# Second half of the tokens by Strassen's seven products: an attention and MLP kernel on one core

## The chip, the cores and the metric

One core of a Trainium2 chip (trn2) runs the whole program in one launch. The metric is device microseconds of an execution, the median of several. TensorE (PE in the profile) multiplies; VectorE (DVE) and ScalarE (ACT) move, round and add; SyncE (SP) issues every DMA; GpSimd (POOL) works in the attention only.

## The reference

The attention's output, 1792 tokens of 768 numbers, goes through two layers. This is the part that the change touches:

```python
def _moe_ref(x, w1, w2, w3, w_out):      # x: 1792 x 768
    a = x @ w1                           # w1, w2: 768 x 1024
    b = x @ w2
    h = a * b @ w3                       # w3: 1024 x 1024
    return (h @ w_out).astype(np.float32)   # w_out: 1024 x 768

def _moe2_ref(x, w_in, w_out):
    h = x @ w_in                         # w_in: 768 x 2048
    g = np.maximum(0.01 * h, h)
    return (g @ w_out).astype(np.float32)   # w_out: 2048 x 768
```

The weights arrive as float64. They are read as pairs of 32-bit words.

## The kernel before

The attention fills the first 409.6 us and leaves x in DRAM (`scr`). The rest is `moe()`, twice over: the tokens are taken in two halves of T = 896 columns (4 batches of S = 448 tokens, two to a half), and everything below is kept with the tokens along the columns.

Exact products come from a split. Every operand is kept as a rounded part hi (`hi_act`, one ScalarE copy) and the rest lo (`lo_dve`, one VectorE subtraction), and each 128-row block of a product is three matmuls: hi·hi, hi·lo, lo·hi. `mm` (its matmul is L619) does this for one block of 128 rows of a weight matrix against all k blocks, in the two column parts of `PARTS`, 512 and 384 columns. Each part is one PSUM bank; there are 8 banks for everything.

One half of the tokens is these stages:

- w1 and w2: 8 row blocks m each, 6 k blocks. A block of w1 and the same block of w2 make a block of h = a·b (copy on ScalarE, L684; product on VectorE, L686).
- w34: the product of w3 and w_out, made once in the first half by `fold` (L530) and stored in DRAM. 6 row blocks of 8 k blocks turn h into x2.
- four groups f: four row blocks of w_in (6 k blocks) make g with the leaky relu (L702, L704), and then the second product (L716) with four row blocks of w_out2: 14 PSUM tiles (7 row groups t of 128 tokens, 2 column halves) of 12 matmuls of 384 columns. They are added up on VectorE in `acc` (L723), and after the last f each t is stored to `out`.

The weights flow through one list, `plan`, which holds the order of all blocks for both halves. `fill` issues loads up to three ahead (buffers `wr`), `convert` turns float64 words into float32 (one ScalarE operation, four on VectorE: L92, L93, L96, L99; buffers `wc`, two), and `split` makes hi and lo (`ws`). A weight block needed in both halves is loaded as float64 and converted twice. While the last second product of the first half runs, `next_x` loads x of the second half and splits it.

Within `moe()` a scheduler orders the instructions of each engine. SyncE's queue is in order: a DMA that waits for a buffer holds those behind it.

Of the kernel before, what the change touches and what calls it, by code (L numbers as in the profile page):

```python
# [8 lines left out]
F32 = mybir.dt.float32  # L9
# [13 lines left out]
def attention_moe_kernel(ctx: ExitStack, tc, qt, kt, vt, w_pre, w_post, w1, w2, w3t, w_out, w_in2, w_out2, out):  # L23
# [37 lines left out]
    w34 = dram.tile([DF, DM], F32, name="w34")  # L61

# [23 lines left out]
    def convert(pool, t, shape):  # L86

        c = pool.tile([P, *shape], U32, tag="wc", name="wc", bufs=2)
# [392 lines left out]
    def moe():  # L481
        with ExitStack() as es:
            xp = es.enter_context(tc.tile_pool(name="m_x", bufs=1, reuse_waits="tile"))
            cv = es.enter_context(tc.tile_pool(name="m_cv", bufs=2, reuse_waits="tile"))
            wp = es.enter_context(tc.tile_pool(name="m_raw", bufs=3, reuse_waits="tile"))
            sp = es.enter_context(tc.tile_pool(name="m_split", bufs=3, reuse_waits="tile"))
            hg = es.enter_context(tc.tile_pool(name="m_hg", bufs=1, reuse_waits="tile"))
            ap = es.enter_context(tc.tile_pool(name="m_acc", bufs=1, reuse_waits="tile"))
            so = es.enter_context(tc.tile_pool(name="m_so", bufs=4, reuse_waits="tile"))
            wk = es.enter_context(tc.tile_pool(name="m_wk", bufs=2, reuse_waits="tile"))  # L490

            KM, KF, KF2 = DM // P, DF // P, DF2 // P
            T = 2 * S
            NT = T // P
            NH = DM // 2
            FQ = 4
            XREADS, XMARKS = (-5, -3), (-5, -5, -4, -4, -4, -4, -3, -3, -3, -2, -2, -2)
            PARTS = ((0, 512), (512, T - 512))

            def behind(mark):  # L500
                es = ExitStack()
                for e in mark.values():
                    es.enter_context(tc.issue_after(e.ins))
                return es

            wos = {}

            def wo_parts(kk):

                if kk < 4:  # L510
                    t = so.tile([P, 2, DM], F32R, tag="ws", name="wo")
                    wos[kk] = t[:, 0], t[:, 1]
                    return wos[kk]
                if kk == 4:
                    t = ap.tile([P, NT, DM], F32R, tag="acc", name="wo")
                    extra = ap.tile([P, DM], F32R, tag="wx", name="wo")
                    for i in range(4, KF):
                        wos[i] = t[:, 2 * i - 8], (t[:, 2 * i - 7] if i < KF - 1 else extra)
                return wos[kk]

            def fold():

                for f in range(KF):
                    wt = next_w()
                    for hf in range(2):
                        cs = slice(hf * NH, (hf + 1) * NH)
                        pw = bank([P, NH], "pw")
                        for kk in range(KF):
                            for j, (x, y) in enumerate(((0, 0), (0, 1), (1, 0))):
                                nc.tensor.matmul(  # L530
                                    pw, wt[:, x, kk, :], wos[kk][y][:, cs],
                                    start=(kk == 0 and j == 0), stop=(kk == KF - 1 and j == 2),
                                )
                        o = wk.tile([P, NH], F32, tag="at", name="wfo")
                        nc.scalar.activation(out=o, in_=pw, func=ACTF.Copy)
                        nc.sync.dma_start(out=w34[f * P:(f + 1) * P, cs], in_=o)

            def col_block(w, m):
                return w[:, 2 * m * P:2 * (m + 1) * P].rearrange("(k p) m -> p k m", p=P)

            def load_w(kind, m):
                if kind == "w34":
                    t = wp.tile([P, KF, P], F32, tag="wr", name="wf", bufs=3)
                    nc.sync.dma_start(out=t, in_=w34[:, m * P:(m + 1) * P].rearrange("(k p) m -> p k m", p=P))
                    return t
                if kind == "wf":
                    return load_raw(wp, w_out[m * P:(m + 1) * P, :].unsqueeze(1), (1, DM), 3)
                if kind == "wo":
                    return load_raw(wp, w_out2[m * P:(m + 1) * P, :].unsqueeze(1), (1, DM), 3)
                if kind == "w3t":  # L550
                    f, i = divmod(m, 2)
                    rows = w3t[i * KF // 2 * P:(i + 1) * KF // 2 * P]
                    return load_raw(wp, col_block(rows, f), (KF // 2, P), 3)
                w = {"w1": w1, "w2": w2, "wi": w_in2}[kind]
                return load_raw(wp, col_block(w, m), (KM, P), 3)

            def ready_w(kind, m, t):
                if kind == "w34":
                    shape, cf = (KF, P), t
                else:  # L560
# [38 lines left out]
            def prepare(ahead):  # L599
                while len(ready) < ahead and pos[1] < len(plan):  # L600
                    fill()
                    if not loaded:
                        return
# [177 lines left out]
```

## Time and profile before

| | |
|---|---|
| median of 3 runs | 1294.88 us (1294.81 to 1299.5) |
| the profiled execution's own time | 1296.19 us |
| its span, first to last instruction | 1294.4 us |
| TensorE busy | 1279.2 us, 99% of the span |
| TensorE weight loads busy (beside the matmuls) | 1127.2 us, 87% |
| VectorE busy | 867.4 us, 67% |
| ScalarE busy | 601.9 us, 46% |
| moved by DMA | 211.57 MB, mean 163 GB/s |

The profiled execution ran 1.3 us longer than the median; 1.8 us of its time lie outside the span. A share of busy time is a mean over the whole program; what an engine does in one stage is read from a table of windows.

### The profile page before, as it was taken

The page shows a single profiled execution, that of the slowest core. Times are in us where ns is not written, and L with a number is a line of the kernel's source. Part 1 is how long each engine was busy: PE and PEld are TensorE (multiplying, and loading weights), DVE is VectorE, ACT ScalarE, POOL GpSimd, SP SyncE. Part 2 cuts the span into 40 slices and gives each one's busy share as a digit, 9 for nine tenths or more (in the row PEclk, how much of TensorE's full clock was granted, in tenths as well). Part 3 has the DMA queues.
Part 4 walks back from the last instruction along what each step waited for, and adds up shares of the span by engine and source line. Part 5 has one row for each costly group of instructions (what it writes and reads, how often), then busy time and mean ns, then how long its engine had stood idle before and what let it go on. Part 6 is the DMA issues. An engine that isn't in the chain of part 4 may idle for free.

```text
span 1294.4 us, 22410 instructions
## 1 busy us (share of the span) xinstructions
PE 1279.2 (99%) x8926; PEld 1127.2 (87%) x8926; DVE 867.4 (67%) x1441; ACT 601.9 (46%) x1169; POOL 117.3 (9%) x192
## 2 busy tenths in 40 slices
PE   7899999999999999999999999999999999999998
PEld 5577777777778989999899999999898889999998
DVE  4565675675668999833485969695673459687662
ACT  5665666676655554522254524352332236434240
POOL 1232232232321000000000000000000000000000
PEclk8899999999999999999999999999999999999999
DMA  7998988988885654733334423363321424342302
GB/s 221 302 319 228 268 261 268 285 266 226 256 261 168 185 163 142 228 115 88 123 105 140 126 95 122 98 218 127 119 82 49 133 77 149 98 147 74 123 1 86
DMA packets 132072, 211.57 MB, mean 163 GB/s; under 512 B 19393, under 2 KB 115649, under 8 KB 131521
## 3 DMA queue, kind: packets, MB, share of 16 engines
q1 hardware_dynamic: 131969, 210.15, 52.6%
q8 instruction: 71, 1.16, 0.4%
q14 instruction: 32, 0.26, 0.1%
HBM read 157.43 MB, written 52.69 MB: 162 GB/s over the span
## 4 chain that ended last, share of the span: by engine, by line
PE 96%; DMA 3%; DVE 1%; ACT 0%; issue 0%; SPq 0%; DVEq 0%
PE pm L619 45%; PE po L716 18%; PE po L304 11%; PE pm L261 6%; PE px L324 6%; PE pw L530 5%; PE pq L203 4%; DMA sr<-sdr 2%; DMA vs<-in_v_dram 1%; PE turn L242 1%; DMA sdr<-s 0%; DVE wc L96 0%; DVE x L75 0%; ACT s L211 0%; DVE ap L311 0%
## 5 line engine op out<-in xcount | busy, mean ns | idle before, releaser
L619 PE MATMUL pm<-x,ws 128*128 128x512 f32 (+1 forms) x2304 | 467.0, 364 | 0.2 <-ACT ws L72 0.2
L619 PEld LDWEIGHTS pm<-x,ws 128*128 128x128 f32 x2304 | 417.6, 188 | 48.0 <-ACT ws L72 0.3
L716 PE MATMUL po<-ws,g 128*128 128x384 f32 x1344 | 234.3, 334 | 0.0
L716 PEld LDWEIGHTS po<-ws,g 128*128 128x128 f32 x1344 | 233.1, 188 | 0.0
L304 PE MATMUL po<-kr,e 128*112 128x120 f32 (+1 forms) x1440 | 159.7, 270 | 0.0
L277 ACT ACTIVATE e<-pm,mx 128x448 f32<-128x448 f32 x180 | 111.8, 632 | 100.0 <-DVE mx L270 99.6
L304 PEld LDWEIGHTS po<-kr,e 128*112 128x112 f32 x1440 | 151.2, 178 | 7.5 <-issue 6.3
L75 DVE TENSOR_TENSOR ws<-wc,ws 128x768 fp32r<-128x768 f32 (+1 forms) x112 | 102.5, 918 | 69.6 <-ACT ws L72 69.0
L72 ACT ACTIVATE ws<-wc 128x768 fp32r<-128x768 f32 (+1 forms) x112 | 90.8, 813 | 113.6 <-PE po L716 73.9
L91 ACT ACTIVATE wc<-wr 128x768 f32<-128x768 f32 (+1 forms) x120 | 104.9, 877 | 78.0 <-DVE ws L75 57.5
L290 POOL TENSOR_SCALAR kr<-kpost,rc 128x120 f32<-128x120 f32 x180 | 113.1, 644 | 276.2 <-DVE rc L287 144.4
L311 DVE COPY ap<-po 112x480 f32<-112x480 f32 (+1 forms) x129 | 83.8, 653 | 55.8 <-PE po L304 55.4
L270 DVE TENSOR_REDUCE mx<-pm 128x1 f32<-128x448 f32 x180 | 101.2, 618 | 25.0 <-PE pm L261 24.6
L619 PE MATMUL pm<-h,ws 128*128 128x512 f32 (+1 forms) x576 | 116.3, 363 | 0.0
L619 PEld LDWEIGHTS pm<-h,ws 128*128 128x128 f32 x576 | 104.3, 188 | 11.7
L99 DVE SCALAR_TENSOR_TENSOR wc<-wr,wc 128x768 uint32<-128x768 uint32 (+1 forms) x120 | 110.3, 920 | 1.6
L96 DVE SCALAR_TENSOR_TENSOR wc<-wr,wc 128x768 uint32<-128x768 uint32 (+1 forms) x120 | 110.0, 919 | 0.9
L261 PE MATMUL pm<-sr,kpre 60*64 60x448 f32 (+1 forms) x720 | 86.0, 567 | 7.0 <-DMA sr<-sdr 6.9
L92 DVE TENSOR_SCALAR wc<-wc 128x768 f32<-128x768 f32 (+1 forms) x120 | 64.8, 540 | 37.9 <-ACT wc L91 37.4
L324 PEld LDWEIGHTS px<-ap,vs 112*64 112x64 f32 x1536 | 73.9, 137 | 17.1 <-ACT e L277 8.2
L723 DVE TENSOR_TENSOR acc<-po,acc 128x384 f32<-128x384 f32 x84 | 46.2, 557 | 62.1 <-PE po L716 61.3
L211 ACT ACTIVATE s<-pq 120x448 f32<-120x448 f32 (+1 forms) x180 | 84.1, 560 | 4.7 <-PE pq L203 4.0
(54 smaller groups left out, 952.8 us busy)
## 6 DMA issues: line engine op xcount, KB each, us to landing
sr<-sdr SPq DMA_DIRECT2D x176, 210.0 KB
wr<-in_moe_w_out_dram SPq DMA_DIRECT2D x40, 768.0 KB
sdr<-s SPq DMA_DIRECT2D x33, 840.0 KB
wr<-in_moe_w_dram SPq DMA_DIRECT2D x32, 768.0 KB
wr<-in_moe_w_in_dram SPq DMA_DIRECT2D x32, 768.0 KB
wr<-in_moe_w_dram SPq DMA_DIRECT2D x16, 512.0 KB
sdr<-s SPq DMA_DIRECT2D x12, 616.0 KB
wf<-w SPq DMA_DIRECT2D x12, 512.0 KB
```

The source lines that it names most:

```text
L75: nc.vector.tensor_tensor(out=dst, in0=src, in1=hi.bitcast(F32), op=ALU.subtract)
L91: nc.scalar.activation(out=cf, in_=hi.bitcast(F32), func=ACTF.Abs)
L96: nc.vector.scalar_tensor_tensor(out=c, in0=hi, scalar=0xC0000000, in1=c, op0=ALU.bitwise_and, op1=ALU.bitwise_or)
L99: nc.vector.scalar_tensor_tensor(out=c, in0=lo, scalar=29, in1=c, op0=ALU.logical_shift_right, op1=ALU.bitwise_or)
L261: nc.tensor.matmul(pms[n][g * Q:(g + 1) * Q], kpre[rows], sr[rows, g, :], start=True, stop=True)
L270: nc.vector.tensor_reduce(out=mxs[n], in_=pms[n], axis=AX.X, op=ALU.max, negate=True)
L277: ends["act"] = nc.scalar.activation(out=ets[n], in_=pms.pop(n), func=ACTF.Exp, bias=mxs.pop(n), scale=1.0, accum_out=sm[:, i:i + 1])
L290: ends["pool"] = nc.gpsimd.tensor_scalar(out=kr[:, i], in0=kpost, scalar1=rc[:, i:i + 1], scalar2=None, op0=ALU.mult)
L304: nc.tensor.matmul(po[:, jc].rearrange("p h (g i) -> p h g i", g=2), e[:, jc * JP:(jc + 1) * JP], kr, start=True, stop=True,)
L324: nc.tensor.matmul(px[e * D:(e + 1) * D, r, :ni], vst[b][:, jc, 2 * p + e, :], ap[:, jc, 2 * p + e, :ni], start=(jc == 0), stop=(jc == NJ ...
L619: nc.tensor.matmul(dst, wt[:, a, kk, :], x[:, kk, c, c0:c0 + w], start=(kk == 0 and j == 0), stop=(kk == kn - 1 and j == 2),)
L716: nc.tensor.matmul(po, g[:, m, a, t * P:(t + 1) * P], wts[m][:, c, 0, cs], start=(m == 0 and j == 0), stop=(m == FQ - 1 and j == 2),)
```

## The change

Of the second half only, the products with w1, w2 and w_in are done by Strassen's scheme in the form with fifteen additions. Weights are taken as 2 x 2 blocks: two row blocks m0, m1 by two halves of the k blocks (3 each). x is taken as 2 x 2 blocks: two halves of the k blocks by the two batches of 448 columns. `seven` makes seven products of 3 k blocks (9 matmuls of 448 columns) where the plain way needs eight. Four of the seven multiply sums: S1 to S4 of weight blocks and t1 to t4 of x blocks. The seven results are put together by seven additions on VectorE (`partial`, `put_block`).

Where these sums come from: those of w1 and w2 are made in the first half, beside the w34 stage (`four_sums` on float32 blocks read back from DRAM, stored again to `summed`). Those of w_in are made in the second half on VectorE, inside the stages that multiply with w_in. The sums of x are made beside the last second product of the first half, those of x2 beside the w34 stage of the second half.

The first half now stores each converted block of w1, w2, w_in and w_out2 as float32 (`kept`, 48 stores of 393 KB), and the second half loads those and converts nothing. `convert` has three buffers `wc` for two. Second half: w34 and the second products keep their number of matmuls; w34 is taken in parts of 448 and 448 columns. A weight tile `w7` of the new scheme holds 7 blocks in hi and lo and has 2 buffers; the first half's pools are closed and the second half's opened inside the last second product.

The diff, cut to its core (the first half is indented and otherwise as it was, apart from the lines shown):

```diff
-        c = pool.tile([P, *shape], U32, tag="wc", name="wc", bufs=2)
+        c = pool.tile([P, *shape], U32, tag="wc", name="wc", bufs=3)
...
+                    if kind in kept:
+                        nc.sync.dma_start(out=kept[kind][m], in_=cf.rearrange("p k m -> p (k m)"))
...
+        def four_sums(u, a11, a12, a21, a22):
+            tt(u[:, 0], a21, a22, ALU.add)
+            tt(u[:, 2], a11, a21, ALU.subtract)
+            tt(u[:, 1], u[:, 0], a11, ALU.subtract)
+            tt(u[:, 3], a12, u[:, 1], ALU.subtract)
...
                 for m in range(KM):
                     wt = next_w()
+                    for part in PARTS:
+                        put(xx[m], mm(wt, h, KF, part), *part)
+                    for kind, m0 in (pairs.pop(0) for _ in range(min(len(pairs), 2 - m // 2 % 2))):
+                        a, u = (so.tile([P, 4, KH * P], F32, tag="ws", name=n) for n in ("sa", "su"))
+                        for i in range(2):
+                            nc.sync.dma_start(out=a[:, 2 * i:2 * i + 2], in_=halves_of(kind, m0 + i * KF // 2))
+                        four_sums(u, *(a[:, i] for i in range(4)))
+                        nc.sync.dma_start(out=summed[kind, m0], in_=u)
...
+                def weights(kind, m0, m1):
+                    w = wb.tile([P, 7, 2, KH, P], F32R, tag="w7", name="w7", bufs=2)
+                    ws = w.rearrange("p i x k m -> p i x (k m)")
+                    raw = ws[:, :, 1].bitcast(F32)
+                    for i, m, k in ((A22, m1, 1), (A11, m0, 0), (A12, m0, 1)):
+                        nc.sync.dma_start(out=raw[:, i], in_=halves_of(kind, m)[:, k])
+                    if (kind, m0) in summed:
+                        u = raw[:, 3:]
+                        nc.sync.dma_start(out=u, in_=summed[kind, m0])
+                    else:
+                        u = swp[0].tile([P, 4, KH * P], F32, tag="sw", name="sw")
+                        nc.sync.dma_start(out=u[:, 2], in_=halves_of(kind, m1)[:, 0])
+                        four_sums(u, raw[:, A11], raw[:, A12], u[:, 2], raw[:, A22])
+                    for s, r in ((raw[:, :3], slice(0, 3)), (u, slice(3, 7))):
+                        hi_act(ws[:, r, 0], s)
+                        lo_dve(ws[:, r, 1], s, ws[:, r, 0])
+                    return w
...
+                def product(w, i, b):
+                    dst = bank([P, S], "pp")
+                    for kk in range(KH):
+                        for j, (a, c) in enumerate(TERMS):
+                            nc.tensor.matmul(dst, w[:, i, a, kk, :], b[:, kk, c, :], ...
...
+                def seven(w, b, put_block):
+                    x1 = product(w, A11, b11)
+                    nc.scalar.activation(out=p1, in_=x1, func=ACTF.Copy)
+                    x5 = product(w, S1, t1)
+                    put_block(0, 0, product(w, A12, b21), p1)
+                    u2 = partial("u2", product(w, S2, t2), p1)
+                    u4 = partial("u4", x5, u2)
+                    u3 = partial("u3", product(w, S3, t3), u2)
+                    put_block(1, 1, x5, u3)
+                    put_block(1, 0, product(w, A22, t4), u3)
+                    put_block(0, 1, product(w, S4, b22), u4)
...
+                            seven(ready.pop(0), x, put_a)
+                            ahead(2 if m < KF // 2 - 1 else 1)
+                            seven(ready.pop(0), x, put_h)
...
+                    for m in range(FQ // 2):
+                        seven(ready.pop(0), x2, put_g)
```

How it moves instructions is shown at three places. In the rows after the change, line numbers are those of the changed kernel: L805 is the matmul of `product`, L515 that of `mm`, L79 makes lo (`lo_dve`), L543 is an addition or subtraction (`tt`), L537 the addition to `acc`, L944 the leaky relu; `pp` is a PSUM tile of `product`, `t_...` the sums of x, `b_...` its plain blocks, `w_...` a weight tile `w7`.

TensorE, second half: before, the first blocks of w1 and w2 (and all 32 such rows up to the w34 stage).

```order
L619 MATMUL pm<-x,ws 128x512 x18
L619 MATMUL pm<-x,ws 128x384 x18
L619 MATMUL pm<-x,ws 128x512 x18
L619 MATMUL pm<-x,ws 128x384 x18
```

And now the third weight tile of w1 and w2; 8 tiles make this stage, 8 more the w_in stages.

```order
L805 MATMUL pp<-b_9096,w_9481 128x448 x9
L805 MATMUL pp<-t_9099,w_9481 128x448 x9
L805 MATMUL pp<-b_9097,w_9481 128x448 x9
L805 MATMUL pp<-t_9100,w_9481 128x448 x9
L805 MATMUL pp<-t_9101,w_9481 128x448 x9
L805 MATMUL pp<-t_9102,w_9481 128x448 x9
L805 MATMUL pp<-b_9098,w_9481 128x448 x9
```

Two row blocks were 4 groups of 18; they are 7 groups of 9, so 63 matmuls of 448 columns for 72 of 448 on average.

VectorE, from the last second product of the first half to the first products of the second: before.

```order
L75 TENSOR_TENSOR x<-x 128x448 x3
L723 TENSOR_TENSOR acc<-po,acc 128x384
L75 TENSOR_TENSOR x<-x 128x448
L75 TENSOR_TENSOR ws<-wc,ws 128x768
L96 SCALAR_TENSOR_TENSOR wc<-wr,wc 128x768
...
L723 TENSOR_TENSOR acc<-po,acc 128x384 x3
L75 TENSOR_TENSOR ws<-wc,ws 128x768
L92 TENSOR_SCALAR wc<-wc 128x768
L93 TENSOR_SCALAR wc<-wc 128x768
L686 TENSOR_TENSOR ht<-pm,at 128x512
```

The same place now, its last rows up to the first addition of a product.

```order
L537 TENSOR_TENSOR acc<-po,acc 128x384
L79 TENSOR_TENSOR t_9102<-gt,t_9102 128x448
L79 TENSOR_TENSOR w_9472<-w_9472 128x4x384
L537 TENSOR_TENSOR acc<-po,acc 128x384 x2
L79 TENSOR_TENSOR t_9101<-gt,t_9101 128x448
...
L79 TENSOR_TENSOR t_9100<-u_9183,t_9100 128x448
L543 TENSOR_TENSOR gt<-b_9097,u_9183 128x448
L537 TENSOR_TENSOR acc<-po,acc 128x384 x2
L79 TENSOR_TENSOR b_9097<-b_9097 128x3x448
L79 TENSOR_TENSOR w_10185<-w_10185 128x1024
L79 TENSOR_TENSOR t_9102<-gt,t_9102 128x448
L543 TENSOR_TENSOR u_9430<-pp,p_9396 128x448
```

The 12 splits of x became 12 sums (L543), 12 splits of sums (L79, 448 wide) and 3 splits of plain blocks (3x448 wide), and the last of them stands directly ahead of the first product's addition.

VectorE in the stage of w_in, third group f: before, a stretch of one row block.

```order
L704 TENSOR_TENSOR gg<-pm,gt 128x512
L93 TENSOR_SCALAR wc<-wc 128x768
L75 TENSOR_TENSOR ws<-wc,ws 128x768
L96 SCALAR_TENSOR_TENSOR wc<-wr,wc 128x768
L75 TENSOR_TENSOR g<-gg,g 128x512
```

Now, at the end of the first of the group's two weight tiles.

```order
L543 TENSOR_TENSOR gt<-pp,u_11564 128x448
L79 TENSOR_TENSOR g<-gt,g 128x448
L944 SCALAR_TENSOR_TENSOR gt<-gt 128x448
L543 TENSOR_TENSOR sw<-sw,w_11727 128x384
L543 TENSOR_TENSOR sw<-w_11727,sw 128x384
L543 TENSOR_TENSOR sw<-sw,w_11727 128x384
L79 TENSOR_TENSOR g<-gt,g 128x448
L543 TENSOR_TENSOR sw<-w_11727,sw 128x384
L79 TENSOR_TENSOR w_11727<-w_11727 128x3x384
L543 TENSOR_TENSOR gt<-pp,p_11631 128x448
```

The four sums of the next group's weights (`sw`) stand in VectorE's order between the steps that make g. They need loads that SyncE can issue only when the tile `w_11727` reuses is free, that is after the last matmul of the seven just ended.

## Rows read from the trace of the kernel before

**Rows 1.** The page's engines: busy time, share of the span, instructions.

```profile
PE 1279.2 (99%) x8926; PEld 1127.2 (87%) x8926; DVE 867.4 (67%) x1441; ACT 601.9 (46%) x1169; POOL 117.3 (9%) x192
```

**Rows 2.** Timeline of PE, start and length in us, after the attention.

```profile
409.58 102.07 PE L619 MATMUL pm<-x,ws 128*128 128x512 f32 x504 [0.17 <-ACT ws L72]
511.49 66.72 PE L530 MATMUL pw<-wo,ws 128*128 128x384 f32 x384
592.58 58.16 PE L619 MATMUL pm<-h,ws 128*128 128x512 f32 x288
854.21 29.28 PE L716 MATMUL po<-ws,g 128*128 128x384 f32 x168
883.33 116.43 PE L619 MATMUL pm<-x,ws 128*128 128x512 f32 x576
999.59 58.16 PE L619 MATMUL pm<-h,ws 128*128 128x512 f32 x288
...
1261.22 29.29 PE L716 MATMUL po<-ws,g 128*128 128x384 f32 x168
```

**Rows 3.** Waits of PE from 400 us to the end.

```profile
PE pm L619 <- ACT ws L72: 0.2, 1, 0.2
```

**Rows 4.** Groups by line of the second half, 883.3 to 1294.4 us.

```profile
L619 PE MATMUL pm<-x,ws 128*128 128x384 f32 (+1 forms) x1152 | 233.3, 364 | 0.0
L716 PE MATMUL po<-ws,g 128*128 128x384 f32 x674 | 117.6, 334 | 0.0
L619 PE MATMUL pm<-h,ws 128*128 128x512 f32 (+1 forms) x288 | 58.2, 363 | 0.0
```

**Rows 5.** Timeline of PE in the attention, around two waits.

```profile
16.73 3.01 PE L203 MATMUL pq<-ks,qs 64*120 64x448 f32 x28
...
24.31 5.20 PE L261 MATMUL pm<-sr,kpre 60*64 60x448 f32 x16 [3.92 <-DMA sr<-sdr]
...
42.02 4.15 PE L261 MATMUL pm<-sr,kpre 60*64 60x448 f32 x16 [3.00 <-DMA sr<-sdr]
```

**Rows 6.** Windows there: us, engines' busy time, granted clock, DMA share, GB/s.

```profile
22.00:24.00 2.00, 0.00 (x0) 0.00 (x0) 0.00 (x0) 0.00 (x0) 0.00 (x0) 0.66 0.82 217
24.00:26.00 2.00, 1.69 (x8) 0.64 (x8) 0.00 (x0) 0.00 (x0) 0.00 (x0) 0.50 0.89 207
...
32.00:34.00 2.00, 2.00 (x18) 0.62 (x16) 0.58 (x2) 0.98 (x2) 1.70 (x4) 0.78 0.92 312
...
42.00:44.00 2.00, 1.99 (x10) 0.75 (x12) 0.62 (x1) 0.26 (x1) 0.00 (x0) 0.78 0.97 309
...
48.00:50.00 2.00, 2.00 (x11) 1.44 (x10) 0.07 (x1) 1.56 (x4) 1.76 (x4) 0.51 1.01 250
50.00:52.00 2.00, 2.00 (x21) 2.00 (x21) 0.66 (x1) 0.81 (x2) 0.50 (x1) 1.00 0.98 371
```

**Rows 7.** Windows by stage, same columns: PE, PEld, DVE, ACT, POOL.

```profile
409.60:511.50 101.90, 101.90 (x505) 91.39 (x506) 95.56 (x142) 53.54 (x74) 0.00 (x0) 1.00 0.56 173
...
592.60:650.60 58.00, 58.00 (x290) 52.14 (x289) 26.21 (x35) 15.29 (x22) 0.00 (x0) 1.00 0.32 102
...
883.30:999.60 116.30, 116.30 (x579) 104.42 (x578) 64.96 (x90) 38.73 (x57) 0.00 (x0) 1.00 0.27 83
```

**Rows 8.** Timeline of VectorE beside the last second product of the first half.

```profile
861.94 0.63 DVE L75 TENSOR_TENSOR x<-x 128x448 fp32r<-128x448 f32 x1 [1.31 <-ACT x L72]
...
869.29 2.23 DVE L75 TENSOR_TENSOR x<-x 128x448 fp32r<-128x448 f32 x4
...
873.77 1.49 DVE L723 TENSOR_TENSOR acc<-po,acc 128x384 f32<-128x384 f32 x3
```

**Rows 9.** Timeline of ScalarE there: the two loads of x.

```profile
861.33 2.92 ACT L72 ACTIVATE x<-x 128x448 fp32r<-128x448 f32 x6 [3.55 <-DMA x<-scr]
...
865.73 2.92 ACT L72 ACTIVATE x<-x 128x448 fp32r<-128x448 f32 x6 [0.75 <-DMA x<-scr]
```

**Rows 10.** Groups by line, second half, VectorE: conversion and split of weights.

```profile
L75 DVE TENSOR_TENSOR ws<-wc,ws 128x768 fp32r<-128x768 f32 x45 | 43.0, 957 | 43.5 <-ACT ws L72 43.4
L99 DVE SCALAR_TENSOR_TENSOR wc<-wr,wc 128x768 uint32<-128x768 uint32 x43 | 41.0, 954 | 0.5
```

**Rows 11.** Waits of SyncE's queue, 409.6 to 515 us: total, times, longest.

```profile
SPq L83 <- DVE wc L99: 94.3, 24, 6.2
```

**Rows 12.** Timeline of the last microseconds (the span ends at 1294.4).

```profile
1290.54 0.56 DVE L723 TENSOR_TENSOR acc<-po,acc 128x384 f32<-128x384 f32 x1 [1.53 <-PE po L716]
1291.13 0.33 SPq L726 DMA_DIRECT2D out_dram<-acc  x1
```

More of the change, by code (lines that the diff above doesn't have):

```diff
@@ new lines, in put, with mm @@
+        def put(dst, src, c0, w):
+            hi_act(dst[:, 0, c0:c0 + w], src)
+            lo_dve(dst[:, 1, c0:c0 + w], src, dst[:, 0, c0:c0 + w])
+        def mm(wt, x, kn, part, order=None):
+            c0, w = part
+            dst = bank([P, w], "pm")
+            order = order or list(range(kn))
+            for kk in order:
+                for j, (a, c) in enumerate(TERMS):
+                    nc.tensor.matmul(
+                        dst, wt[:, a, kk, :], x[kk][:, c, c0:c0 + w],
+                        start=(kk == order[0] and j == 0), stop=(kk == order[-1] and j == 2),
+                    )
+            return dst
@@ new lines, in tt, with halves_of @@
+        def tt(dst, x, y, op):
+            nc.vector.tensor_tensor(out=dst, in0=x, in1=y, op=op)
+        def halves_of(kind, m):
+            return kept[kind][m].rearrange("p (k c) -> p k c", k=2)
+        def four_sums(u, a11, a12, a21, a22):
[3 more added lines that the diff above has]
+            tt(u[:, 3], a12, u[:, 1], ALU.subtract)
+        summed = {
+            (kind, m): dram.tile([P, 4, KH * P], F32, name=f"sums_{kind}_{m}")
+            for kind in ("w1", "w2") for m in range(KF // 2)
+        }
@@ L625, in put, with fill @@
[L625 to L629 removed]
+                pos = [0, 0]
+                loaded, ready, halved, folded = [], [], [None], []
+                def fill():
+                    while pos[0] < len(plan) and pos[0] < pos[1] + 3 and (folded or plan[pos[0]][0] != "w34"):
+                        loaded.append(load_w(*plan[pos[0]]))
+                        pos[0] += 1
@@ new lines, in prepare, with next_w @@
+                def prepare(ahead):
+                    while len(ready) < ahead and pos[1] < len(plan):
+                        fill()
+                        if not loaded:
+                            return
+                        w = ready_w(*plan[pos[1]], loaded.pop(0))
+                        pos[1] += 1
+                        fill()
+                        if w is not None:
+                            ready.append(w)
+                def next_w(ahead=2):
+                    prepare(ahead)
+                    return ready.pop(0)
@@ L728, in attention_moe_kernel @@
+        first_half()
     attention()
```

474 lines of the change are left out of this document (291 added, 183 removed).

## The prediction

> **What bounds the kernel now.** I read the page's list of engines first: TensorE is busy in 99% of the span, VectorE in 67%, ScalarE in 46% [rows 1]. A mean over all stages could hide a stage that another engine sets, so TensorE's timeline after the attention came next: from 409.58 us on each stage begins where the one before it ends, up to the last second product at 1261.22 [rows 2], and the table of its waits has one line, 0.2 us [rows 3]. So after 410 us the time is the number of matmuls times their spacing, plus the last 3.3 us (last addition and last store). What the change does to other engines counts only where it makes TensorE wait. That needs the slack of VectorE stage by stage [rows 7]: it has 6.3 us in the first half's stage of w1 and w2 (95.56 of 101.9), 32 us beside w34, 51 us in the second half's w1 and w2.
>
> **Matmuls taken away.** In the second half the products with w1, w2 and w_in are 1152 matmuls [rows 4], half of 512 and half of 384 columns, 448 on average. The change makes 16 weight tiles of 63, that is 1008, all of 448 columns. The 288 of w34 go from 512 and 384 to 448 and 448; the 672 of the second products stay.
>
> The spacing comes from a stage without waits: 576 matmuls in 116.43 us [rows 2] are 0.2021 us for a mean of 448 columns. The 384-wide ones of the second product take 29.28/168 = 0.1743 [rows 2], so the 512-wide take 2 × 0.2021 − 0.1743 = 0.2299. No full 448-wide row stands in the trace; its ends are these two, 0.1743 and 0.2299. Both are columns/2400 plus some 0.015 us (0.160 + 0.014, 0.2133 + 0.0166), so 448 columns should take 0.1867 + 0.0155 = 0.202, and I take 0.2021. Then w34 costs what it did, and the gain is 144 × 0.2021 = **29.1 us**.
>
> A nearer row bounds it from above. In the attention, 28 matmuls of 448 columns that fill 64 rows take 3.01 us [rows 5], 0.1075 each; if two of them share the array, as I assume, a pair lasts 0.215. At that spacing (1008 + 288) × 0.215 = 278.6 replaces 233.3 + 58.2 = 291.5 [rows 4], a gain of 12.9.
>
> The Trainium skill (TensorE: Matmul & The Clock Gate, section Back-to-back issue gap) gives columns / 2.4 + 2.5 ns as the isolated spacing at full clock, 189 ns for 448 columns and the same 189 as the mean of 512 and 384. This trace measures 202 for that mean, so the rows decide; by the rule the gain would be 144 × 0.189 = 27.2, an estimate, 1.9 less.
>
> **First half: stores and the first sums.** 48 stores of 393 KB, 16 loads of 393 KB and 8 stores of 786 KB are 31.5 MB. VectorE gets 32 subtractions or additions of 384 columns, at 1.49/3 = 0.50 us (three of that width [rows 8]) 16 us, all in the w34 stage where it is busy 26.21 of 58 us [rows 7]: 42 of 58, hidden; if the cover were gone they would cost 16. The new wait is that of a conversion for its buffer: `wc` is free only after the store has landed. A store of 384 KB takes 3.3 us from its issue (1291.13) to the end of the span (1294.4) [rows 12]. With three buffers two other conversions lie in between, each four operations and a split of VectorE, some 4 us at 0.95 for the dearest steps [rows 10]. SyncE already stands waiting for the same event: it waited 94.3 us in 24 times for the conversion's last step [rows 11]. So the store goes out at once and lands in time: cost 0 to 1, taken as 0.
>
> **Boundary of the halves.** Beside the last second product (29.28 us, 854 to 883 before) VectorE now has 24 operations of 448 columns at 2.23/4 = 0.56 [rows 8], 13.4; three of 1344 at the same rate, 5.0; weights of 1152 and 1536 columns for two tiles, 5376 columns at 0.957/768 [rows 10], 6.7; 1024 of w34, 1.3; and 14 additions to acc, 7.0. Sum 33.4. It starts when x has landed: the second of two loads (1376 KB) came 4.4 us behind the first (865.73 − 861.33 [rows 9]), 313 GB/s. The four half loads of 688 KB, issued now at the end of the last w_in block, take 2.2 us each; with at most 3.3 us to land [rows 12] the first two are there some 6 us after the second product's begin, and VectorE, with two additions to acc already behind it, ends at about 6 + 33.4 − 1 = 38. TensorE asks for the last of it late: the order of its first seven leaves 8 of the 9 matmuls with b21 and the last two with t4 to the end, some 55 matmuls in, 29.3 + 55 × 0.2021 = 40.4. A margin of 2.4; I take a stall of **1 us** (0 to 5).
>
> **Stages of the second half.** w1, w2: a seven lasts 63 × 0.2021 = 12.7 us. Per pair of weight tiles VectorE has 14 additions, 4 products, 4 splits of h and 5376 columns of weights: 22 × 0.56 + 6.7 = 19 of 25.5 us. Loads of a tile are issued when the seven that held it ends, a whole seven (12.7 us) before use, 1.4 MB in 4.4 us plus 3.3 plus the split: some 3 to 5 us to spare. w34: first load close, later ones with 3 us; **0.5 us**. w_in: VectorE stands at the sums `sw` until loads issued at the end of the seven land, at most 3.3 us [rows 12]; meanwhile TensorE goes on with the next seven or the finished parts of the second product in eight banks. I take 0.25 for each of four groups, **1 us**. That conversions vanish (43 blocks [rows 10] of four operations) gains nothing, since VectorE was not waited for. The tail is the same.
>
> **Sum.** The profiled execution took 1296.19: − 29.1 + 1 + 0.5 + 1 = 1269.6. The median of the runs is 1.3 lower, so **1268**.
>
> **Rivals.**
> 1. *Boundary late.* The DMA shares 7 MB there, and stretches of 207 GB/s exist [rows 6]. At that rate x and the first tiles land 5 us later than at 313, past the margin: a stall of 3 to 5 us. A stall has a second price: after waits of 3.92 and 3.00 us [rows 5] the granted clock went to 0.50, the 1.2 GHz level, and was back at 1.00 within the window of 32 to 34 us, 10 us later [rows 6], which loses up to 5.1 us. Together 5 + 4: **1277**. For it: VectorE full for 33 us; against it: the order keeps the late operands for the end.
> 2. *448 columns cost more than the mean of 512 and 384.* At 0.215 the gain is 12.9, stalls alike: 1296.19 − 12.9 + 2.5 − 1.3 = **1284**. Against it: both measured widths follow one line. The forecast turns to a loss only above 291.5/1296 = 0.2249.
> 3. *Weights of w_in late.* If the eight banks don't cover the hold at `sw`, each of the three group boundaries with loads behind it costs 3.3 us and a half clock of about 3.4 (half of the 6.8 us from 43.2 to 50 after the wait of 3.00 [rows 6]): 3 × 6.7 = 20, **1288**. A margin of 2.5 to 3 us stands against it. VectorE's rows show in-order work: it waited 1.31 us for ScalarE's part of x [rows 8] with additions to acc behind it. The Trainium skill (same page, section Architectural detail: the array is 16× 32×32, not 1× 128×128) says that only TensorE takes instructions ahead, weight loads, while ScalarE and VectorE are strictly first in, first out. By that rule everything behind a late `sw` waits, as this rival has it; the row agrees, and no row here shows the hold itself.
> 4. *Slower than before: stores hold up conversions in the first half.* Place: 409 to 511 us, where VectorE has 6.3 us of slack [rows 7] and 14 blocks of w1 and w2 are stored. If every landing of 3.3 us lay bare, 14 × 3.3 − 6.3 = 39.9 would go against a gain of 26.6: **1308**. It decides from (26.6 + 6.3)/14 = 2.35 us for each stored block. Against it: the third buffer, and DMA busy at 0.56 there.
> 5. *The change doesn't do what it says:* the order has 1008 matmuls of 448 columns; only their price is open, as in 2.
>
> **Chances.** Forecast 0.70 (its own range 1264 to 1273), rival 1 0.11, rival 2 0.05, rival 3 0.08, rival 4 0.06. What a measurement of this kernel can tell from no change is about 0.5%, 6.5 us: 1288.4 to 1301.4. Rival 3 lies at that bound; 0.02 of it counts as faster, 0.06 as the same. Faster: 0.70 + 0.11 + 0.05 + 0.02 = 0.88; same 0.06; slower 0.06. The range goes from 1263 (no stall anywhere, 448 columns a little under the line) to 1284, which takes in rivals 1 and 2 and leaves out 0.14 above.
>
> **What would show it.** The second half's w1 and w2 should be 504 matmuls in 102 us (from 116.43), each w_in stage 126 in 25.5 (from 29.2), w34 288 in 58.2. TensorE's waits should hold a few lines of 1 us or less: at the first seven for x's sums, at the first w34 block. The granted clock should stay at 1.00 after 410 us; a stretch at 0.50 behind a wait of VectorE or of a DMA is rival 1 or 3, told apart by its place. VectorE ought to be busy more in 854 to 893 and less elsewhere in the second half. 409 to 511 should keep its 102 us; longer means rival 4. A seven clearly over 12.9 us without waits would be rival 2.

## The result and the profile after

The changed kernel takes 1277.19 us (median of 4 runs, 1274.22 to 1278.79) against 1294.85 us of before (4 runs): ratio 0.9854, 95% interval 0.9823 to 0.9884. It is faster by 1.5%, inside the range that was predicted and 9 us above the predicted time. The profiled execution took 1278.79 us with a span of 1277.0, so 17.4 us less span than before.

The page of the changed kernel, busy time of each engine (beside [rows 1]):

```profile
PE 1257.7 (98%) x8782; PEld 1111.0 (87%) x8782; DVE 863.4 (68%) x1461; ACT 566.2 (44%) x1104; POOL 117.4 (9%) x192
```

TensorE's waits from 400 us on (beside [rows 3]) are two, in the first microseconds after the attention. None stands in the second half:

```profile
PE pm L515 <- ACT ws L76: 1.1, 1, 1.1
PE pm L515 <- DVE ws L79: 1.1, 1, 1.1
```

TensorE's timeline of the changed kernel (start, length; the stages of [rows 2], and one of the groups of products):

```profile
411.44 2.02 PE L515 MATMUL pm<-x,ws 128*128 128x512 f32 x8 [1.10 <-ACT ws L76]
414.53 100.39 PE L515 MATMUL pm<-x,ws 128*128 128x512 f32 x496 [1.07 <-DVE ws L79]
514.76 68.00 PE L596 MATMUL pw<-wo,ws 128*128 128x384 f32 x384
...
597.11 58.75 PE L515 MATMUL pm<-h,ws 128*128 128x512 f32 x288
...
859.34 29.29 PE L530 MATMUL po<-ws,g 128*128 128x384 f32 x168
888.47 2.02 PE L805 MATMUL pp<-b,w 128*128 128x448 f32 x9
...
907.07 5.74 PE L805 MATMUL pp<-t,w 128*128 128x448 f32 x27
...
992.62 59.68 PE L515 MATMUL pm<-h,w 128*128 128x448 f32 x288
1052.14 2.02 PE L805 MATMUL pp<-b,w 128*128 128x448 f32 x9
...
1078.18 29.29 PE L530 MATMUL po<-wo,g 128*128 128x384 f32 x168
...
1243.66 29.29 PE L530 MATMUL po<-wo,g 128*128 128x384 f32 x168
```

From start to start of the stages, in us:

| stage | before | after | difference |
|---|---|---|---|
| attention, until its last product ends | 409.41 | 410.33 | +0.9 |
| handover, the two waits | 0.17 | 2.18 | +2.0 |
| first half's first w1, w2 blocks, without the waits | 101.91 | 102.25 | +0.3 |
| fold | 66.56 | 67.84 | +1.3 |
| first half's w34 | 58.00 | 58.59 | +0.6 |
| second half's w1, w2 | 116.27 | 104.16 | −12.1 |
| second half's w34 | 58.00 | 59.52 | +1.5 |
| four stages of w_in | 116.27 | 104.14 | −12.1 |
| all the rest, the tail included | | | +0.2 |

The three rows of the second half that change give 22.7 us, where 29.1 was forecast. TensorE waits for nothing there: 504 matmuls in 104.16 us and 288 in 59.52 are both 0.2067 us each. The first half gives back 4.2 us where 0 was forecast. The 0.9 us of the attention is no effect of the change: over 13 profiles of this study (all but that of experiment 7) its last 160 products begin anywhere from 400.46 to 406.97 us. From the attention's end to the program's end, on the other hand, the changed kernel takes 866.7 us in this profile and again in that of experiment 9. So profiles are compared from there on below; that the attention is also most of why the totals of one kernel scatter by several us is likely, but not shown run by run.

### The profile page after: what moved, and what is told of

It is laid out like the page before. It is cut to its first block, busy times and chain, and to the rows that moved or that the text cites. A ratio compares the mean times of both kernels' runs of the same rounds, so it can differ in the third digit from the quotient of the medians.

```text
span 1277.0 us, 22314 instructions
## 1 busy us (share of the span) xinstructions
PE 1257.7 (98%) x8782; PEld 1111.0 (87%) x8782; DVE 863.4 (68%) x1461; ACT 566.2 (44%) x1104; POOL 117.4 (9%) x192
## 4 chain that ended last, share of the span: by engine, by line
PE 95%; DMA 4%; DVE 1%; SPq 0%; issue 0%; ACT 0%; DVEq 0%
PE pm L515 27%; PE po L530 18%; PE pp L805 16%; PE po L308 11%; PE px L328 6%; PE pm L265 6%; PE pw L596 5%; PE pq L207 4%; DMA sdr<-s 1%; DMA sr<-sdr 1%; DMA vs<-in_v_dram 1%; DMA kl<-in_k_dram 0%; PE turn L246 0%; DVE wc L103 0%; DVE wc L100 0%; SPq L254 0%
## 5 line engine op out<-in xcount | busy, mean ns | idle before, releaser
L515 PE MATMUL pm<-x,ws 128*128 128x384 f32 (+1 forms) x1152 | 234.0, 364 | 2.2 <-ACT ws L76 1.1
L515 PEld LDWEIGHTS pm<-x,ws 128*128 128x128 f32 x1152 | 208.7, 188 | 26.6 <-ACT ws L76 1.5
L805 PE MATMUL pp<-t,w 128*128 128x448 f32 x576 | 124.5, 368 | 0.0
L274 DVE TENSOR_REDUCE mx<-pm 128x1 f32<-128x448 f32 x180 | 101.1, 618 | 25.7 <-PE pm L265 25.5
L805 PEld LDWEIGHTS pp<-t,w 128*128 128x128 f32 x576 | 108.1, 188 | 10.9
L530 PE MATMUL po<-ws,g 128*128 128x384 f32 x672 | 117.2, 334 | 0.0
L530 PE MATMUL po<-wo,g 128*128 128x384 f32 x672 | 117.2, 334 | 0.0
L530 PEld LDWEIGHTS po<-wo,g 128*128 128x128 f32 x672 | 116.6, 188 | 0.2
L530 PEld LDWEIGHTS po<-ws,g 128*128 128x128 f32 x672 | 116.6, 188 | 0.0
L805 PE MATMUL pp<-b,w 128*128 128x448 f32 x432 | 95.6, 368 | 0.0
L537 DVE TENSOR_TENSOR acc<-po,acc 128x384 f32<-128x384 f32 x84 | 45.7, 557 | 67.1 <-PE po L530 66.9
L805 PEld LDWEIGHTS pp<-b,w 128*128 128x128 f32 x432 | 81.0, 188 | 8.0
L328 PE MATMUL px<-ap,vs 112*64 112x120 f32 (+1 forms) x1536 | 84.7, 265 | 2.3 <-DMA vs<-in_v_dram 2.3
```

The lines of the kernel that those rows point to most:

```text
L274: nc.vector.tensor_reduce(out=mxs[n], in_=pms[n], axis=AX.X, op=ALU.max, negate=True)
L328: nc.tensor.matmul(px[e * D:(e + 1) * D, r, :ni], vst[b][:, jc, 2 * p + e, :], ap[:, jc, 2 * p + e, :ni], start=(jc == 0), stop=(jc == NJ ...
L515: nc.tensor.matmul(dst, wt[:, a, kk, :], x[kk][:, c, c0:c0 + w], start=(kk == order[0] and j == 0), stop=(kk == order[-1] and j == 2),)
L530: nc.tensor.matmul(po, g[m][:, a, t * P:(t + 1) * P], wts[m][:, c, cs], start=(m == 0 and j == 0), stop=(m == FQ - 1 and j == 2),)
L805: nc.tensor.matmul(dst, w[:, i, a, kk, :], b[:, kk, c, :], start=(kk == 0 and j == 0), stop=(kk == KH - 1 and j == 2),)
```

## The experiments

**1. The width alone.** Is it the 448 columns that cost more, or the new operand tiles? In the kernel before:

```diff
-            PARTS = ((0, 512), (512, T - 512))
+            PARTS = ((0, S), (S, S))
```

> The kernel before, with its token columns cut 448 and 448 in place of 512 and 384 in every product that mm makes (2880 matmuls); nothing else is changed. Theory A: the width itself is dear, 448 columns take 206.7 ns wherever they stand, as in the changed kernel, against a mean of 201.9 for 512 and 384. Then each stage of w1 and w2 in the second half takes 576 x 0.2067 = 119.0 us (116.3 before), w34 59.5 (58.0), and the whole 2880 x 0.0048 = 14 us more, about 1309 us. Rival B: the 206.7 come from the new operand tiles or weight tiles of the seven products; then 448 columns cost 0.202 here and the time stays at 1295.

Measured: 1307.63 us (4 runs, 1307.55 to 1307.83) against 1295.77; ratio 1.0091, interval 1.0074 to 1.0108. Its timeline of TensorE:

```profile
408.84 102.48 PE L619 MATMUL pm<-x,ws 128*128 128x448 f32 x504
...
887.66 119.20 PE L619 MATMUL pm<-x,ws 128*128 128x448 f32 x576
1006.70 59.68 PE L619 MATMUL pm<-h,ws 128*128 128x448 f32 x288
```

The second half is what theory A said: 119.2 and 59.7 us, 0.2067 each from start to start, with the old tiles and no Strassen. Rival B falls. But the first stage does not follow: 504 of the same matmuls take 102.48, 0.203 each. Read one by one, its starts lie some 199 to 207 ns apart in a repeating pattern with a mean of 202.7 behind the first two; after `fold` nearly every step is 206 or 207. This first stage begins 0.14 us behind the attention's last product, the later ones follow other matmuls without a pause. So a stream of 448 columns has two spacings, and something sets which.

**2. Where the columns begin.** The same with rows of x and x2 padded:

```diff
-                x = xp.tile([P, KM, 2, T], F32R, tag="x", name="x")
+                x = xp.tile([P, KM, 2, 1024], F32R, tag="x", name="x")
...
-    out=x[:, :, 1, n * S:(n + 1) * S]
+    out=x[:, :, 1, n * 512:n * 512 + S]
```

> As the kernel before with 448 and 448 columns, but the tiles of x and x2 have rows of 1024 in place of 896 words, so that each part of 448 columns begins at a multiple of 2048 bytes; h and g stay. Theory A (width): 206.7 ns for w1, w2 and w_in as without the padding. Rival C (the address at which the 448 columns begin): w1, w2 and w_in fall to 200 to 202 ns (116 us for the second half's w1 and w2), w34 alone stays at 206.7.

Measured: 1306.54 us (one run). The second half's w1 and w2 in its timeline:

```profile
886.61 119.19 PE L619 MATMUL pm<-x,ws 128*128 128x448 f32 x576
```

That is 206.7 ns each from start to start, as without padding. Rival C falls.

**3. Other widths.**

```diff
-            PARTS = ((0, 512), (512, T - 512))
+            PARTS = ((0, 480), (480, T - 480))
+            PARTS_H = ((0, 496), (496, T - 496))
+            PARTS_G = ((0, 464), (464, T - 464))
...
```

> The kernel before with other cuts: w1 and w2 480 and 416 columns, w34 496 and 400, w_in 464 and 432. It tells the price by width. If the surcharge over columns/2400 goes in steps (13.3 ns at 384 and 512, 20.0 at 448), the pairs cost 2 x 0.2020 where both widths have the low step and 2 x 0.2067 where both have the high one: a stage of w1 and w2 between 116.3 and 119.0 us, w34 between 58.0 and 59.5, w_in between 29.1 and 29.8. If 448 is a single dear width, all three stay at the low end.

Measured: 1301.25 us (one run), of which the attention alone ended 4.7 us later than in the profile of before. The stages of its second half (w1 and w2, w34, the first of w_in):

```profile
888.21 116.52 PE L621 MATMUL pm<-x,ws 128*128 128x480 f32 x576
1004.57 58.30 PE L621 MATMUL pm<-h,ws 128*128 128x496 f32 x288
1062.70 29.25 PE L621 MATMUL pm<-x,ws 128*128 128x464 f32 x144
```

They stand at the low end: 116.4, 58.1 and 29.1 us from start to start. Mean distances between starts: 400 columns 180.5 ns, 416 186.9, 432 193.7, 464 209.8, 480 217.4, 496 223.2; 384 has 173.3 in second products and 512 some 229. Every pair of 896 columns costs what 512 and 384 do, so there is no step of the price between 384 and 512; of the cuts tried, only 448 twice is dear. But these pairs change the width every 18 or 24 matmuls, while 448 twice is one unbroken stream. Of the other widths only 384 ran in a long stream by itself, so whether 432 or 464 alone could be caught at a dearer spacing is not shown.

**4. What stands ahead of the stream.** The changed kernel, with a matmul ahead of eight of the groups of seven that writes into the PSUM tile and is overwritten:

```diff
+                short = [0, 32, 0, 64, 0, 128, 0, 256, 128, 0, 256, 0, 192, 0, 320, 0]
+
-                def product(w, i, b):
+                def product(w, i, b, n=0):
                     dst = bank([P, S], "pp")
+                    if n:
+                        nc.tensor.matmul(dst[:, :n], w[:, i, 0, 0, :], b[:, 0, 0, :n], start=True, stop=True)
...
-                    x1 = product(w, A11, b11)
+                    x1 = product(w, A11, b11, short.pop(0))
```

> The changed kernel with one more matmul, which adds nothing to the result, ahead of some of the 16 groups of seven products: of 32, 64, 128 and 256 columns ahead of the 2nd, 4th, 6th, 8th of the w1 and w2 stage, of 128, 256, 192 and 320 ahead of the first of each w_in pair. With 448 columns in the kernel before, the stream ran at 202.6 ns until fold, having begun after an idle TensorE, and at 206.7 after the 384-wide matmuls of fold. Theory P (the spacing of 448 columns depends on how the stream stands against its weight loads, and is kept once taken): at one of the widths the stream changes to 202.6 ns and keeps it, up to 5 us less for the rest, and at most 0.2 us for each added matmul. Rival F: 206.7 is what 448 columns cost here, whatever precedes; the spacing stays 206.7 and the kernel gets 1 to 2 us longer.

Measured: 1273.83 us (one run). Its timeline around the first short one, at 900.05 us:

```profile
889.31 2.02 PE L809 MATMUL pp<-t,w 128*128 128x448 f32 x9
...
900.05 0.18 PE L806 MATMUL pp<-b,w 128*128 128x32 f32 x1
...
900.56 1.99 PE L809 MATMUL pp<-b,w 128*128 128x448 f32 x9
...
906.03 5.63 PE L809 MATMUL pp<-t,w 128*128 128x448 f32 x27
```

27 matmuls that took 5.74 us before now take 5.63. Start to start, the seven ahead of 900 us has 206.6 ns and all that follow have 202.7, w34 and the four w_in stages too (58.4 and 25.7 us, start to start). The short matmul of 32 columns itself costs 0.1 us: 0.03 to the next start, and the next one's 0.28 in place of 0.20. Rival F falls. Theory P holds so far as a spacing, once taken, is kept; that it comes from how the stream stands against its weight loads is not shown, for at both spacings a weight load begins 2 to 4 ns behind the start of a matmul.

**5. Third conversion buffer.** The changed kernel with

```diff
-        c = pool.tile([P, *shape], U32, tag="wc", name="wc", bufs=3)
+        c = pool.tile([P, *shape], U32, tag="wc", name="wc", bufs=2)
```

> The changed kernel with two conversion buffers wc in place of three, as before the change. In the profile of the changed kernel VectorE works on a third conversion between the steps of the first two, the first splits end some 2 to 3 us later, and TensorE waits 1.1 and 1.07 us at 411 us. Theory W (the third buffer's early conversion delays the first weights): the two waits go, the program gets some 2 us shorter than the changed kernel, near 1275. Rival S (the stores need the third buffer): with two buffers each conversion waits for the store of the last but one; the stage from 410 to 515 us grows by 0.5 us or more for each of some 14 stored blocks, 7 us or more, and the whole ends above 1280.

Measured: 1276.7 us (5 runs, 1273.65 to 1277.79). VectorE's timeline at the handover, first of the changed kernel (three buffers), then of this one:

```profile
406.10 0.55 DVE L97 TENSOR_SCALAR wc<-wc 128x768 uint32<-128x768 uint32 x1
406.56 0.55 DVE L96 TENSOR_SCALAR wc<-wc 128x768 f32<-128x768 f32 x1
407.03 1.82 DVE L100 SCALAR_TENSOR_TENSOR wc<-wr,wc 128x768 uint32<-128x768 uint32 x2
...
411.54 0.95 DVE L100 SCALAR_TENSOR_TENSOR wc<-wr,wc 128x768 uint32<-128x768 uint32 x1
...
412.65 0.95 DVE L103 SCALAR_TENSOR_TENSOR wc<-wr,wc 128x768 uint32<-128x768 uint32 x1
413.52 1.83 DVE L79 TENSOR_TENSOR ws<-wc,ws 128x768 fp32r<-128x768 f32 x2
```

```profile
409.05 1.82 DVE L103 SCALAR_TENSOR_TENSOR wc<-wr,wc 128x768 uint32<-128x768 uint32 x2
410.79 0.33 DVE L337 COPY y<-px 128x176 f32<-128x176 f32 x1
411.04 1.81 DVE L79 TENSOR_TENSOR ws<-wc,ws 128x768 fp32r<-128x768 f32 x2
```

With three buffers a third block's steps (L96 at 406.56, L100 at 411.54, L103 at 412.65) stand ahead of the splits that TensorE waits for; with two they don't, the splits begin 2.5 us earlier, and TensorE's table of waits is empty. From the attention's end to the program's end the profile gives 864.3 us for 866.7, 2.3 less, as theory W has it; the medians (1276.7 for 1277.19) don't resolve it under the attention's scatter. The first stage takes 101.96 us with two buffers: the stores hold nothing up. Rival S falls.

**6. Operands in memory.** The kernel before with the pools of h and g, of acc and of the four w_out tiles placed from the other end (the first of three lines alike):

```diff
-            hg = es.enter_context(tc.tile_pool(name="m_hg", bufs=1, reuse_waits="tile"))
+            hg = es.enter_context(tc.tile_pool(name="m_hg", bufs=1, side="right", reuse_waits="tile"))
```

> The kernel before with three pools (h and g, acc, the four w_out tiles) placed from the other end of the on-chip memory, as in the changed kernel's first half; no instruction is changed. In the changed kernel the 384-wide matmuls of fold took a steady 176.6 ns (173.3 before), whatever VectorE and the DMA did beside them. Theory L: the place of the operands in memory sets it; fold then takes 67.8 us here as well (66.6 before). Rival T: the traffic of the new stores and loads; fold stays at 66.6.

Measured: 1298.15 us (one run). Its timeline has the changed kernel's fold and more than its w34:

```profile
510.04 68.00 PE L530 MATMUL pw<-wo,ws 128*128 128x384 f32 x384
...
592.39 59.19 PE L619 MATMUL pm<-h,ws 128*128 128x512 f32 x288
```

TensorE runs the same matmuls in the same order as before, where these took 66.72 and 58.16 [rows 2]. Theory L holds: the 1.3 us of fold come from where its operands lie. In w34 the moved h costs 1.0 us here. The changed kernel moves only half of h (k blocks 4 to 7), and its trace tells the halves apart, under the same traffic: with the half that stayed, w34's matmuls of 512 columns lie 228.3 ns apart on average (230.1 before), with the moved half 234.6 (226.7 before). So its 0.6 us come from the place as well.

**7. Both ends exchanged** in the changed kernel (the default side "right", the three named ones "left").

> The changed kernel with the two ends of the on-chip memory exchanged for all its pools; no instruction is changed. The kernel before with three pools at the other end had fold at 176.7 ns in place of 173.3 and w34 at 233.4 and 176.5 in place of 228.4 and 174.4. Theory L (it is the distance or order of the two operands in memory): exchanged, the first half's fold and w34 return to 66.6 and 58.0 us (67.8 and 58.6 in the changed kernel), 2 us less. Rival: the absolute address counts; then fold takes either value and the second half's products may change too.

Measured: 1298.43 us (one run), and not usable as a whole: TensorE waited 18.3 us at the handover for x, whose tile now lies where the attention still works. Its fold:

```profile
534.15 68.00 PE L596 MATMUL pw<-wo,ws 128*128 128x384 f32 x384
```

From start to start fold took 67.8 us and w34 58.8, and the second half's 448-wide matmuls kept 206.7 ns. So exchanging the ends doesn't restore the old spacing. It reverses the order of the two operands and leaves them at opposite ends, so it speaks against the order and not against the distance. In all these traces the matmuls that got slower are those whose weights and moving operand lie in pools at opposite ends; what it is about the addresses that does it is open.

**8. Later weights.** The changed kernel with

```diff
+                    if (kind, m0) not in summed:
+                        nc.sync.dma_start(out=raw[:, 0:4], in_=summed["w1", 0])
                     for i, m, k in ((A22, m1, 1), (A11, m0, 0), (A12, m0, 1)):
```

> The changed kernel with one more load of 786 KB into each weight tile of w_in, ahead of its own loads and overwritten by them, so that these land some 4 us later. The prediction gave TensorE 2.5 to 3 us of cover in the w_in stages, and the changed kernel shows no wait there. If that cover is right, waits of 1 to 2 us appear at the group boundaries, each perhaps with a stretch at half clock: 5 to 15 us in all. If the cover is far larger, as the rival has it, nothing is waited for and the time stays.

Measured: 1278.01 us (one run). VectorE's wait for these weights in the w_in stages (total, times, longest), in the changed kernel and then here:

```profile
DVE sw L543 <- DMA w<-kept_wi: 4.0, 4, 2.0
```

```profile
DVE sw L543 <- DMA w<-kept_wi: 12.3, 5, 3.5
```

TensorE waited for none of it, so its cover in these stages is over 3.5 us. It did wait twice in w34, beside which the first two tiles of w_in are made and whose second block's load stood behind the added ones. TensorE's timeline there and in the first w_in stage, and windows around the two waits:

```profile
991.56 10.08 PE L515 MATMUL pm<-h,w 128*128 128x448 f32 x48
1002.29 1.09 PE L515 MATMUL pm<-h,w 128*128 128x448 f32 x4 [0.65 <-ACT w L76]
1003.93 48.09 PE L515 MATMUL pm<-h,w 128*128 128x448 f32 x236 [0.55 <-DVE w L79]
...
1057.34 5.63 PE L807 MATMUL pp<-t,w 128*128 128x448 f32 x27
```

```profile
1000.00:1004.00 4.00, 2.80 (x13) 1.89 (x12) 1.82 (x3) 2.42 (x3) 0.00 (x0) 1.00 0.75 235
1004.00:1008.00 4.00, 4.00 (x20) 3.72 (x21) 3.80 (x6) 2.39 (x3) 0.00 (x0) 1.00 0.25 71
```

The granted clock stayed at 1.00, and the 448-wide stream, 206.7 ns ahead of the waits, had 202.7 behind them until the second product: here an idle moment did what the short matmul does.

**9. Few short matmuls, and both gains.** Three kernels on one chip: the changed kernel unaltered, the same with five short matmuls, and these with two conversion buffers.

```diff
+                short = [32] + 7 * [0] + 4 * [32, 0]
```

> The changed kernel once more, unaltered, beside the two others. Its second half should show 206.7 ns for every 448-wide matmul, fold 67.8 us and the two waits of 2.2 us in all, as in its first profile; its total 1274 to 1279. If the spacing of 448 columns changes from one execution to the next, it shows here as a lower value in some stage.

> The changed kernel with one matmul of 32 columns, which adds nothing to the result, ahead of five groups of seven products: the first of the w1 and w2 stage and the first of each of the four w_in stages. Theory P (spacing kept once taken): all 1296 matmuls of 448 columns run at 202.7 ns in place of 206.7, 5.2 us less, minus 5 x 0.1 us: 4.7 us below the changed kernel run beside it, some 1272.5. Rival F: one short matmul at the start is not enough, the gain seen with eleven of them came from some other place; then the spacing is 206.7 in at least a part of the stages and the gain under 2 us.

> The five short matmuls together with two conversion buffers in place of three. If the two effects add up, 4.7 + 2 us less than the changed kernel, some 1270.5, faster than all kernels so far; the first weights' waits at 411 us (2.2 us) are gone and the 448-wide stages stand at 202.7 ns. If they don't add up, about 1272.5.

Measured, against 1295.95 us of before: unaltered 1278.25 (4 runs, 1275.98 to 1279.97; ratio 0.986, 0.9845 to 0.9876); five short ones 1272.22 (4 runs, 1271.84 to 1275.46; 0.982, 0.9804 to 0.9836); both 1270.87 (5 runs, 1269.27 to 1273.29; 0.9802, 0.9788 to 0.9815). (Experiment 4 had eight short matmuls, not eleven.) The unaltered one repeats 206.7 ns in all stages, fold's 67.8 us and the two waits. The five give 6.0 us in the medians, and between the profiles 4.1 from the attention's end on. With two buffers the waits go but for 0.2 us, and the gains add up: 6.4 us between the profiles.

One of the five did harm. In the kernel with five, the timeline of TensorE at the first w_in stage:

```profile
1046.57 0.18 PE L806 MATMUL pp<-b,w 128*128 128x32 f32 x1
...
1052.26 5.74 PE L809 MATMUL pp<-t,w 128*128 128x448 f32 x27
```

Ahead of it w34 had run at 202.7 ns; behind it this stage runs at 206.7. In experiment 4 a matmul of 128 columns at the same place left the stream at 202.7.

**10. Without that one.**

```diff
-                short = [32] + 7 * [0] + 4 * [32, 0]
+                short = [32] + 9 * [0] + 3 * [32, 0]
```

> The changed kernel with two conversion buffers and four short matmuls of 32 columns: ahead of the first group of seven of w1 and w2 and of the 2nd, 3rd and 4th w_in stage, none ahead of the first w_in stage, where with five of them the short one threw the stream from 202.7 back to 206.7 ns. Theory P (what precedes sets the spacing and it is kept as long as the width stays): the first w_in stage keeps the 202.7 of w34, 25.5 us in place of 26.1, and the whole is 0.6 us below the kernel with five, about 1270.3. Rival: the first w_in stage falls to 206.7 for another reason (its operands), and nothing changes.

Measured: 1270.68 us (5 runs, 1269.99 to 1275.56) against 1296.36: ratio 0.9812, 0.9794 to 0.983. The first w_in stage in its timeline:

```profile
1063.16 5.63 PE L809 MATMUL pp<-t,w 128*128 128x448 f32 x27
1068.64 1.98 PE L809 MATMUL pp<-b,w 128*128 128x448 f32 x9
1070.46 29.31 PE L530 MATMUL po<-wo,g 128*128 128x384 f32 x168
```

It keeps the 202.7 ns, and all 1296 matmuls run at it; the rival falls. The gain of 0.6 us shows in that stage; the medians can't resolve it. Against the kernel before, run beside each, this one is 25.7 us shorter, where the changed kernel is 17.7.

## Why the prediction was right, and where its size was off

**What bounds the kernel** was right: but for 2.2 us of waits at 411 us, only TensorE's number of matmuls and their spacing matter after the attention. There are 144 fewer, and the four stages of w_in and that of w1 and w2 shrank by what their matmuls cost.

**The step that was mis-sized is the spacing of 448 columns.** The prediction took 0.2021 us, the mean of 512 and 384 (0.2019 from start to start), and argued from a line through both: "448 columns should take 0.1867 + 0.0155". The trace of the changed kernel shows 0.2067 for each of the 1296. That is 290.5 us (1152 and 288 of before, start to start) against 1296 × 0.2067 = 267.8, a gain of 22.7 for 29.1; 6.4 us, most of the miss. The line itself was sound: the neighbouring widths of experiment 3 (432 with 193.7 ns, 464 with 209.8) lie within 1.5 ns of it, and 448 columns can be had at 202.7 (experiments 4, 9 and 10). What failed is the step from the line to the new stream, that a width has one spacing and keeps it wherever it stands: the rows that it was drawn from change width every 18 matmuls or are 384 wide, and an unbroken stream of 448 columns behind 384-wide matmuls ran at 206.7 (experiment 1, with the old tiles). Why it does stays open. Rival 2 had said that 448 columns could cost more than the mean, with an upper price of 0.215; 0.2067 lies 36% of the way to it, and its sign, a seven clearly over 12.9 us without waits, is there by little: a seven takes 13.02. The 189 ns that the Trainium skill (TensorE: Matmul & The Clock Gate, section Back-to-back issue gap) gives for 448 columns are 14 to 18 ns below both spacings measured.

**The first half was put at 0 and cost 4.2.** Stores and first sums are indeed hidden: VectorE was busy 41.58 of 58.6 us in the w34 stage (42 of 58 forecast), with DMA at 320 GB/s, and TensorE waited for nothing there. Windows of the first w1 and w2 stage and of w34, same columns as [rows 7]:

```profile
411.40:514.80 103.40, 102.29 (x505) 91.37 (x506) 95.39 (x144) 51.90 (x75) 0.00 (x0) 1.00 0.72 232
...
597.10:655.70 58.60, 58.60 (x290) 52.33 (x290) 41.58 (x66) 18.06 (x26) 0.00 (x0) 1.00 0.90 320
```

What cost was not on the list. The third buffer, counted only as a help, let VectorE put a third conversion ahead of splits that TensorE was waiting for: 2.0 us of waits, and 0.3 more in the same stage that go with them (experiment 5). And new pool ends moved operands of fold and w34: 1.3 and 0.6 us (experiment 6).

**The boundary** was worked out well and its stall, put at 1 us, is 0. VectorE's first sum and its last operations there in the changed kernel:

```profile
865.62 0.62 DVE L543 TENSOR_TENSOR u<-t,b 128x448 f32<-128x448 f32 x1 [1.35 <-DMA t<-scr]
...
893.16 1.56 DVE L79 TENSOR_TENSOR b<-b 128x1344 fp32r<-128x1344 f32 x1
894.81 1.23 DVE L79 TENSOR_TENSOR w<-w 128x1024 fp32r<-128x1024 f32 x1
895.95 0.62 DVE L79 TENSOR_TENSOR t<-gt,t 128x448 fp32r<-128x448 f32 x1
```

The last ends at 896.57, 37.2 us after the second product's begin at 859.34 (38 forecast); TensorE takes the last two matmuls with t4 at 901.28. The margin was 4.7, not 2.4. Rival 1's late loads did not come: VectorE's first sum of x began at 865.62, 6.3 us behind the second product's begin (6 forecast). The DMA moved 244 GB/s in that stretch, between the 207 and the 313 that the prediction weighed, as the window of 859.3 to 888.5 us says:

```profile
859.30:888.50 29.20, 29.20 (x171) 29.20 (x170) 24.45 (x38) 15.46 (x20) 0.00 (x0) 1.00 0.68 244
```

**The w_in stages** were put at 1 us and cost 0. The hold of VectorE that rival 3 described is there, four times and 2.0 us at most. The Trainium skill (TensorE: Matmul & The Clock Gate, section Architectural detail: the array is 16× 32×32, not 1× 128×128) has VectorE strictly first in, first out, and the trace agrees: VectorE did nothing else in these holds. TensorE has more cover than the 2.5 to 3 us that the prediction gave it (experiment 8: over 3.5).

**Rival 4** (stores hold up conversions) fell with experiment 5: two buffers are enough. The stage that was to keep its 102 us did get longer, which the prediction would have read as this rival; it was the third buffer.

Added up between the two profiles: 6.4 us from the spacing and 4.2 from the first half, less the 2.5 of stalls that did not come, plus 1.1 of the attention and the table's last row, make the 9.2 us between the 1269.6 forecast for the profiled execution and its 1278.79. That the miss is not larger is partly luck: the first half's price, which was not on the list, and the stalls that were feared partly offset one another.

## What to carry to other kernels

Where TensorE is full, a product of fewer matmuls gains by their spacing at the new width, so that width wants measuring by itself: one run of the old kernel with 448 and 448 columns would have told it. Extra buffers and new pool places are changes of their own: look at what the scheduler moves ahead of the first thing that is waited for. A stream of equal matmuls can be caught at a slow spacing, and one short matmul ahead of it may free it or, as once here, do the opposite; look at the starts of single matmuls, in each stage, before and after.

## What the runs showed of the hardware that was not expected

- 448-column matmuls with a weight load each run at a steady 206.7 ns or in a pattern of some 199 to 207 ns with a mean of 202.7. The state lasted as long as the stream. Streams that followed 384-wide matmuls 173.3 or 173.4 ns apart without a pause ran at 206.7; one that began 0.14 us behind the attention's last products (experiment 1) ran at 202.7.
- A matmul of 32 columns, or two waits of about 0.6 us, changed the state: to 202.7 where the stream was steady, and in one place to 206.7 where it was not. For how the two are chosen no run gives a rule.
- 384-wide matmuls of one stage took 173.3 or 176.7 ns by the place of their operands alone; slower were those with weights and moving operand at opposite ends of the on-chip memory.
- Waits of 0.55 to 1.1 us of TensorE left the granted clock at 1.00.
